# Linear-attention block on one core: the last two heads' numerators computed by tokens and carried in spare columns of the other heads

## The chip, the cores and the metric

The kernel runs on one core of a Trainium2 chip. The metric is the device time of one execution in microseconds (us). A core has five engines that run their own instruction streams: TensorE (PE) for matrix products, VectorE (DVE) and ScalarE (ACT) for elementwise work and reductions, POOL (GpSimd) for the same and for starting transfers, SP (SyncE) for starting transfers. Products land in PSUM, a memory of eight banks that VectorE and ScalarE read.

## The reference

One transformer block over S = 2048 tokens of width D = 640, with H = 32 heads of Dh = 20 and an MLP of width F = 1728:

```python
mod = (_silu(c) @ w_mod).reshape(c.shape[0], 6, 1, -1)
sa, ca, ga, sb, cb, gb = (mod[:, 0], ..., mod[:, 5])
h = _layernorm(x) * (1 + ca) + sa
# attention, on h:
pq = jnp.einsum("bhsd,hdf->bhsf", q, w_phi)             # pk from k alike
phi_q = jnp.concatenate([_softmax(pq), _softmax(-pq)], axis=-1)
kv  = jnp.einsum("bhsf,bhsd->bhfd", phi_k, v)
z   = jnp.einsum("bhsf->bhf", phi_k)
num = jnp.einsum("bhqf,bhfd->bhqd", phi_q, kv)
den = jnp.einsum("bhqf,bhf->bhq", phi_q, z)[..., None] + 1e-6
o = num / den
...
x = x + ga * (o.reshape(B, S, D) @ wo)
h = _layernorm(x) * (1 + cb) + sb
x = x + gb * (square(relu(h @ w1 + b1)) @ w2 + b2)
```

Each head has 40 features: the softmax of 20 values and that of their negatives.

## The kernel before

Tokens are worked in 16 tiles of 128 and in 8 pairs of tiles (256 tokens, `j` = 0 to 7). Large products are made from a high and a low part of each operand in three terms (high by high, high by low, low by high). All of these products, and the plain fp32 ones of `num`, are written by one helper, line 79; all subtractions that make a low part by another, line 89.

The kernel has three stretches. In the first the weights are folded and keys, values and queries are projected. There TensorE is in the order of the code and a scheduler places the other engines' work. At the end, near 255 us, kv and z of all heads are complete. The second is the attention stage, in which every engine's order is the order of the code. The third is the MLP with its `up` products and accumulators.

In the attention stage 30 heads are worked in five groups (`GR`, 0 to 4) of two halves with three heads each: 60 columns of values, and 120 of features. The last two heads are a sixth group of 40 columns of values and 80 of features. The stage does the following.

- `e_prod(t)`, `e_recip(t)` (VectorE, some on POOL) make the inverse of the denominators of tile t, and `e_scale(t)` multiplies the features by them into `ezb` (1280 columns, in one of four buffers): a pass over 1200 columns (line 905) and one over the last 80 (line 910).
- `tr_e(j, groups)` turns `ezb` by TensorE into a bank `te` (20 transposes of 120 columns, and two of 80 for the sixth group) and ScalarE copies it to `ept` (lines 927 and 929).
- `num(j)` multiplies the turned features by the masked kv (`kvd`, products of 64 columns) into three banks `numa`, `numb`, `numc`. The sixth group's kv stands three times side by side (`kv5`), so that its numerators come out in 120 rows of `numc`.
- `num_hi(j)` (ScalarE) and `num_lo(j)` (VectorE from pair 2 on, TensorE with a negative identity and ScalarE before) store `ot`, the numerators' high and low parts.
- `do_wo(j, i, h)` makes half h (384 or 256 columns) of the attention output of tile 2j + i: 16 products into `pwo`, three terms for each of five groups and one stacked product for the sixth, whose weights `WO[5]` hold high, high and low parts one under the other. ScalarE copies the result to `at` (line 986) and starts its transfer to memory.

Pair j's four `do_wo` calls alternate with the turning and the numerators of pair j + 1. VectorE does `e_scale` for tiles two or three further on. Among these stand the last four query tiles' softmax (`q_chain` with `mxq` and the subtraction at line 438 on VectorE, the exponentials `eq` at lines 441 and 442 on ScalarE), the splitting of MLP weights (`w<-rw`, `w<-rawt`, line 1018), and the first layer norm pieces of the MLP (`junk<-xm`, lines 1122 and 1127, and `xx`, line 1146). In the last pair ScalarE makes the MLP's first inputs (`xm`, `h`).

A single PSUM bank `tp` serves `numc`, then the turned MLP inputs; three banks serve `te`, `numa` and `numb`, and four the output products.

Of the kernel before, what the change touches and what calls it, by code (L numbers as in the profile page):

```python
# [15 lines left out]
P = 128  # L16
# [26 lines left out]
    *range(21),  # L43
    *range(11),
    13, 0, 2, 11, 12, 1, 3, 11, 14, 20, 15, 16, 18, 19, 17, 10, 13, 14, 0, 12,
# [7 lines left out]
def kernel(  # L53
# [347 lines left out]

    def proj(nm, t, between=None):
        p = pj(f"p{nm}{t}")
        j, i = divmod(t, 2)
        s = slice(i * P, (i + 1) * P)
        for h, (a, b) in enumerate(CUT):
            terms = []
            for d in range(NC):
                w = W[nm, d]
                terms += three(HT[j][:, d, 0, s], HT[j][:, d, 1, s], w[:, 0, a:b], w[:, 1, a:b])  # L410
            at, hook = 0, None
            if between and h == between[0]:
                at, hook = between[1:]
                mm(p[h][:, : b - a], terms[:at], last=False)
                hook()
            mm(p[h][:, : b - a], terms[at:], first=(at == 0))
        return p
# [42 lines left out]

    def do_q(t, between=None):
        q_out(t, proj("q", t, between=between))

# [25 lines left out]
    def prep_wo(g, ga_b):  # L489
        o, n = GR[g]  # L490
        t = row("s1", f"rwo{g}")
        m = P
        if g < 5:
            nc.gpsimd.memset(t, 0.0)
            for c in range(2):
                nc.sync.dma_start(t[64 * c : 64 * c + 60], wo[o + 60 * c : o + 60 * c + 60])
        else:
            m = 3 * n
            for i in range(3):
                nc.sync.dma_start(t[i * n : i * n + n], wo[o : o + n])  # L500
        w = wslot(f"wo{g}")
        WO[g] = w
        with tc.issue_after(newest(ET_.DVE)):
            nc.vector.tensor_tensor(t[:m], t[:m], ga_b[:m], op=ALU.mult)
        nc.scalar.activation(w[:m, 0], t[:m], AF.Copy)
        lo(w[:m, 1], t[:m], w[:m, 0])
        if g == 5:
            nc.gpsimd.dma_start(w[2 * n : m, 0], w[2 * n : m, 1])

# [17 lines left out]
    def wo_weights(*gs):  # L527
# [190 lines left out]
    for t in range(2, NT - 2):  # L718
# [13 lines left out]
        p = proj("v", t, (1, 0, lambda: t1(j + 1, 4)) if t == NT - 3 else None)  # L732
        if i == 0:
# [16 lines left out]
        if t < NT - POSTPONED:  # L750
            do_q(t, (1, 3, lambda: t1(j + 1, 4, more=LAST_COL.get(t))) if i else None)
# [62 lines left out]
    kv_t = flat(kvtile)  # L814
    kvd = kv_t[:120, :640].rearrange("p (g n) -> p g n", n=P)
    kv5 = kv_t[:80, 640:760]
    def make_z():
# [18 lines left out]

    q_out(q0 + 1, proj("q", q0 + 1, between=(0, 9, make_z)))

# [9 lines left out]

    def kv_out():
        for b, (g0, g1) in enumerate(((0, 4), (4, 5))):  # L850
            nc.scalar.activation(kv_t[:120, P * g0 : P * g1], kvt[b][:120, : (g1 - g0) * P], AF.Copy)
        nc.scalar.activation(
            kv5.rearrange("p (r n) -> p r n", r=3), kvt[1][:80, None, P : P + 40].to_broadcast([80, 3, 40]), AF.Copy
        )

    def kv_masks():
        k = kv_t[:120, : 5 * P].rearrange("p (g n) -> p g n", n=64)
        nc.vector.tensor_tensor(k, k, mask[:, None, :].to_broadcast([120, 10, 64]), op=ALU.mult)
        k = kv5.rearrange("p (r n) -> p r n", r=3)
        nc.vector.tensor_tensor(k, k, mask5[:, None, :].to_broadcast([80, 3, 40]), op=ALU.mult)  # L860

# [37 lines left out]

    def e_scale(t):  # L900
        if t >= NT:
            return
        dn = DN[t]
        EU[t] = EZB[t % 4]
        nc.vector.tensor_tensor(  # L905
            EU[t][:, :1200].rearrange("p (u s h d) -> p s u h d", s=2, h=3, d=DH),
            ET[t][:, :, :600].rearrange("p s (u h d) -> p s u h d", h=3, d=DH),
            dn[:, :, :30].rearrange("p s (u h) -> p s u h", h=3)[:, :, :, :, None].to_broadcast([P, 2, 10, 3, DH]), op=ALU.mult
        )
        nc.vector.tensor_tensor(  # L910
            EU[t][:, 1200:].rearrange("p (s h d) -> p s h d", s=2, d=DH),
            ET[t][:, :, 600:].rearrange("p s (h d) -> p s h d", d=DH),
            dn[:, :, 30:, None].to_broadcast([P, 2, 2, DH]), op=ALU.mult
        )

    def tr_e(j, gs):
        for g in gs:
            o, n = GR[g]
            p = bank(f"te{j}_{g}")
            t = EPT[j, g] = feat("s4", f"ept{j}_{g}")  # L920
            for i in range(2):
                for c in range(2 if g < 5 else 1):
                    a = c * 256 + i * P
                    b, m = (2 * o + 120 * c, 120) if g < 5 else (1200, 80)
                    nc.tensor.transpose(p[:m, a : a + P], EU[2 * j + i][:, b : b + m], ident)
            if g < 5:
                nc.scalar.activation(t[:120], p[:120].rearrange("p (s n) -> p s n", s=2), AF.Copy)
            else:
                nc.scalar.activation(t[:80, 0], p[:80, :256], AF.Copy)

    def num(j):
        OT[j] = ht(f"ot{j}", j)
        ps = [bank(f"numa{j}"), bank(f"numb{j}"), tp(f"numc{j}")]
        for g in range(5):
            for c in range(2):
                mm(ps[g // 2][64 * c : 64 * c + 64, (g % 2) * 256 : (g % 2) * 256 + 256],
                   [(kvd[:, g, 64 * c : 64 * c + 64], EPT[j, g][:120, c])], first=(g % 2 == 0), last=False, skip=True)
# [3 lines left out]
        OT[j, 5] = row("s3", f"ot5_{j}")[:, 80:336].bitcast(F32R)  # L941
# [14 lines left out]
    def num_lo(j):  # L956

        if j >= DIRECT:
            for b, (src, hi, low) in enumerate(num_parts(j)):
                r = GR[5][1] if b == 3 else P  # L960
                lo(low[:r], src[:r], hi[:r])
            return
        for b, (src, hi, _) in enumerate(num_parts(j)):
            r = 120 if b == 3 else P
            nc.tensor.matmul(src, neg[:r, :r], hi, start=False, stop=True, skip_group_check=True)
        for b, (src, _, low) in enumerate(num_parts(j)):
            r = GR[5][1] if b == 3 else P
            nc.scalar.activation(low[:r], src[:r], AF.Copy)

    PWO, AT = {}, {}  # L970

    def do_wo(j, i, h, a=0, b=16):
        t = 2 * j + i
# [11 lines left out]
        if b == 16:  # L985
            nc.scalar.activation(AT[t][:, cs_], PWO[t][h][:, :n], AF.Copy)
# [201 lines left out]
    for j in range(NB):  # L1188
        nxt = j + 1 < NB
        b, c = 2 * j + 5, 2 * j + 6  # L1190
        te_at = (0, 1) if 0 < j < 6 else (1, 2)
        if j == 4:
# [12 lines left out]
        load_e(b + 2)  # L1205
        def te(at):
            for i, gs in enumerate((range(3), (3, 4, 5) if te_at[0] == 0 else (5, 3, 4))):
                if nxt and te_at[i] == at:
                    tr_e(j + 1, gs)

        do_wo(j, 0, 0)
        te(0)
        if j == 5:
            exps(EQ[KEPT + 3])
            q_sums(KEPT + 3)
            e_prod(b)
        do_wo(j, 0, 1)
        if j == 7:
            t2(0, 0)
            t2(0, 1)  # L1220
        te(1)
        if j == 4:
# [12 lines left out]
        if j != 5:  # L1235
            e_recip(b)
            e_scale(b)
        do_wo(j, 1, 0)
        if j == 7:
            t2(0, 2)  # L1240
            t2(0, 3)
        te(2)
        if nxt:
            num(j + 1)
            num_hi(j + 1)
        do_wo(j, 1, 1, 0, 8)
        if j == 7:
# [6 lines left out]
        if not nxt:  # L1254
            do_wo(j, 1, 1, 8, 16)
        if nxt:
            do_wo(j, 1, 1, 8, 11)
            num_lo(j + 1)
            do_wo(j, 1, 1, 11, 16)
        if j == 5:  # L1260
# [511 lines left out]
```

## Time and profile before

| | us |
|---|---|
| median of three runs | 756.05 (755.88 to 756.07) |
| span of the profiled execution | 754.9 |
| TensorE busy | 749.6 |
| VectorE busy | 607.5 |
| ScalarE busy | 458.8 |
| POOL busy | 170.4 |
| kv and z complete (start of the attention stage) | 254 to 255 |
| first `up` product of the MLP | 386.8 |

The span runs from the first to the last instruction in the trace. The granted clock of TensorE is full throughout. In the lines of the timeline the first two numbers are start and duration in us, then engine, line and tiles; a bracket at the end is the idle time ahead and the instruction that ended it, and xN means that N such instructions are put in one row, from the first's start to the last's end.

### The profile page before, as it was taken

To read this page: it belongs to the slowest core of one execution; us is meant where nothing else is said; L and a number is where in the kernel's file an instruction comes from. 1 tells how busy PE (TensorE), PEld (TensorE's weight loads), DVE (VectorE), ACT (ScalarE), POOL (GpSimd) and SP (SyncE) were. 2 spreads that over 40 slices of the span, in tenths; PEclk is the share of its full clock that TensorE was granted. 3 is DMA by queue.
4 is the path that set the end of the run, shared out by engine and by line. 5 is a ranking of instruction groups with operands and counts; after the bars stand their busy time and mean duration, and the time that the engine had idled before them with its cause. 6 is when DMAs were issued, how large, how long until landed. Compare 5 with 4: busy or idle time off the path is not lost.

```text
span 754.9 us, 15404 instructions
## 1 busy us (share of the span) xinstructions
PE 749.6 (99%) x5888; PEld 731.9 (97%) x5888; DVE 607.5 (80%) x1123; ACT 458.8 (61%) x1060; POOL 170.4 (23%) x365
## 2 busy tenths in 40 slices
PE   9999999999999999999999999999999999999998
PEld 9999999999999998998899999999999999999997
DVE  6598987988999899999755768787777776777766
ACT  5767666677863355556677757485574756647431
POOL 3001101011200237646303030132221313213110
PEclk9999999999999999999999999999999999999999
DMA  9811431342432264664777475897677767667461
GB/s 324 336 39 80 155 96 70 106 139 103 138 105 93 71 190 142 143 153 124 173 204 218 121 216 215 278 326 204 185 213 204 205 196 212 191 181 208 132 188 36
DMA packets 58931, 126.70 MB, mean 168 GB/s; under 512 B 7452, under 2 KB 16417, under 8 KB 58857
## 3 DMA queue, kind: packets, MB, share of 16 engines
q1 hardware_dynamic: 38706, 79.41, 32.1%
q0 software_dynamic: 17568, 41.00, 22.0%
q10 hardware_dynamic: 2583, 5.30, 1.9%
q8 instruction: 46, 0.75, 0.5%
q14 instruction: 28, 0.23, 0.1%
HBM read 100.94 MB, written 29.89 MB: 173 GB/s over the span
## 4 chain that ended last, share of the span: by engine, by line
PE 86%; DVE 11%; POOL 1%; issue 1%; ACT 0%; DVEq 0%; POOLq 0%
PE up L79 24%; PE acc L79 18%; PE pk L79 9%; PE pv L79 9%; PE pq L79 8%; PE acc3x L79 5%; PE pwo L79 3%; PE kvp L455 3%; DVE dn L883 3%; DVE scr L881 2%; DVE ezb L905 2%; PE foldk L281 1%; PE ta L363 1%; DVE ot L89 1%; POOL dn L889 1%; PE foldq L281 1%
## 5 line engine op out<-in xcount | busy, mean ns | idle before, releaser
L79 PE MATMUL up<-h,w 128*128 128x256 f32 x1640 | 204.4, 276 | 0.1
L79 PEld LDWEIGHTS up<-h,w 128*128 128x128 f32 x1640 | 196.4, 188 | 0.5 <-DVE h L89 0.3
L1321 ACT ACTIVATE ft<-up,b_t 128x256 f32<-128x256 f32 x104 | 48.9, 471 | 96.0 <-PE up L79 95.6
L79 PE MATMUL acc<-w,ra 128*128 128x384 f32 x452 | 97.5, 335 | 0.0
L79 PE MATMUL pwo<-wo,ot 128*128 128x256 f32 (+3 forms) x512 | 79.9, 311 | 0.4 <-DVE ot L89 0.4
L1322 DVE TENSOR_TENSOR ft<-ft 128x256 f32<-128x256 f32 x104 | 43.8, 421 | 43.0 <-ACT ft L1321 41.4
L79 PEld LDWEIGHTS pwo<-wo,ot 128*128 128x128 f32 (+1 forms) x512 | 74.3, 188 | 3.5 <-issue 2.7
L79 PE MATMUL pq<-wq,hT 128*128 128x384 f32 (+1 forms) x480 | 75.1, 311 | 0.0
L79 PEld LDWEIGHTS acc<-w,ra 128*128 128x128 f32 x452 | 72.7, 188 | 0.9 <-DVE ra L89 0.6
L79 PE MATMUL pk<-wk,hT 128*128 128x384 f32 (+1 forms) x480 | 72.7, 308 | 0.0
L79 PE MATMUL pv<-wv,hT 128*128 128x384 f32 (+1 forms) x480 | 71.6, 306 | 0.0
L79 PEld LDWEIGHTS pq<-wq,hT 128*128 128x128 f32 x480 | 71.0, 188 | 0.6 <-issue 0.2
L79 PEld LDWEIGHTS pk<-wk,hT 128*128 128x128 f32 x480 | 70.5, 188 | 0.4 <-issue 0.2
L79 PEld LDWEIGHTS pv<-wv,hT 128*128 128x128 f32 x480 | 70.0, 188 | 0.0
L89 DVE TENSOR_TENSOR ra<-ft,ra 128x384 fp32r<-128x384 f32 (+2 forms) x86 | 36.8, 449 | 32.7 <-ACT ra L1345 19.4
L1431 POOL DMA_DIRECT2D ring_a<-td_a x34 | 18.5, 544 | 117.1 <-PE acc L79 103.7
L1345 ACT ACTIVATE ra<-ft 128x384 fp32r<-128x384 f32 x48 | 25.2, 526 | 28.5 <-DVE ft L1322 22.4
L79 PE MATMUL acc3x<-w,ra 128*128 128x256 f32 x231 | 39.5, 278 | 0.0
L79 PEld LDWEIGHTS acc3x<-w,ra 128*128 128x128 f32 x231 | 37.2, 188 | 0.0
L1336 DVE TENSOR_TENSOR ft<-ft 128x128 f32<-128x128 f32 x136 | 33.4, 286 | 1.2
L446 DVE TENSOR_REDUCE sk<-ek 128x64 f32<-128x1280 f32 x16 | 23.7, 1483 | 12.4 <-ACT ek L441 10.8
L889 POOL TENSOR_TENSOR dn<-dn,rs_q 128x32 f32<-128x32 f32 x32 | 19.9, 622 | 59.0 <-DVE dn L883 58.7
(264 smaller groups left out, 1458.2 us busy)
## 6 DMA issues: line engine op xcount, KB each, us to landing
ring_c<-td_c POOLq DMA_DIRECT2D x34, 384.0 KB, 4.1
ring_a<-td_a POOLq DMA_DIRECT2D x34, 384.0 KB, 3.5
ring_b<-td_b POOLq DMA_DIRECT2D x34, 256.0 KB, 3.5
esp<-eq SPq DMA_DIRECT2D x12, 640.0 KB, 3.2
el<-esp SPq DMA_DIRECT2D x12, 640.0 KB, 4.4
rw<-in_w SPq DMA_DIRECT2D x23, 320.0 KB, 3.5
wm<-in_w_mod SPq DMA_DIRECT2D x20, 320.0 KB, 3.7
xb<-in_x SPq DMA_DIRECT2D x8, 640.0 KB, 4.0
```

Of the source, the lines that this page charges most:

```text
L79: nc.tensor.matmul(o, a, b, start=first and i == 0, stop=last and i == len(terms) - 1, skip_group_check=skip,)
L89: (eng or nc.vector).tensor_tensor(out_lo, full, hi.bitcast(F32), op=ALU.subtract)
L281: nc.tensor.matmul(p[g // 3][:, (g % 3) * 120 : (g % 3) * 120 + n], r, bd_t[:120, g * 120 : g * 120 + n], start=True, stop=True,)
L446: nc.vector.tensor_reduce(s, heads(flat(e)), axis=AX.X, op=ALU.add)
L455: nc.tensor.matmul(kvp[g // 4][64 * c : 64 * c + 64, a : a + 2 * n].rearrange("p (s n) -> p s n", s=2), v[:, u], e[:, :, o : o + n], start ...
L883: nc.vector.tensor_reduce(dn.rearrange("p s h -> p (s h)"), heads(z), axis=AX.X, op=ALU.add)
L889: nc.gpsimd.tensor_tensor(dn[:, s], dn[:, s], rs[:, 1 - s], op=ALU.mult)
L1321: nc.scalar.activation(r, p, AF.Relu, bias=b1_t[:, f : f + 1])
L1322: nc.vector.tensor_tensor(r, r, r, op=ALU.mult)
L1336: nc.vector.tensor_tensor(t[:, o], t[:, a], t[:, b], op=op)
L1345: nc.scalar.activation(a[:, 0, :3], t[:, :3], AF.Copy)
L1431: nc.gpsimd.dma_start(RING[j, n, r], TD[n][r].bitcast(F32R))
```

## The change

The last two heads' numerators are computed with tokens as rows instead of columns. `e_scale` is split: `e_tail` writes the 80 scaled features of these heads for both tiles of a pair to a tile of its own, `ut`; `e_main` writes the other 1200 to `ezb`, now ten rows of 128 columns of which 120 are used. `tail_turn(j)` turns `ut` into the bank `tail` (the one of `numc`), and ScalarE copies it to `ept_5`. `tail_num(j)` multiplies `ept_5` (as the loaded operand) by the 40 columns of `kv5`, and ScalarE copies the 40 numerators of every token into columns 120 to 123 of the ten rows of `ezb`, four to a row. The `te` transposes take 124 columns, so the numerators are turned with the features. `kvd` gets four rows of an identity for each half, which hand them through `num` into rows 60 to 63 and 124 to 127 of each group's numerators, spare so far. The rows of `wo` for these 40 columns are loaded into the same rows of the five groups' weights. So `WO[5]`, its preparation, its slot, the sixth group's two products in `num`, its high and low parts and the 16th product of every output half are gone. The `hooks` of `do_wo` put the four steps `tail_turn`, `tail_num`, `te` of groups 0 to 2 and `te` of groups 3 and 4 between the output products: `turns` gives for each the tile of the pair, the half and the number of products ahead of it.

```diff
@@ prep_wo @@
-        m = P
-        if g < 5:
-            nc.gpsimd.memset(t, 0.0)
-            for c in range(2):
-                nc.sync.dma_start(t[64 * c : 64 * c + 60], wo[o + 60 * c : o + 60 * c + 60])
-        else:
-            m = 3 * n
-            for i in range(3):
-                nc.sync.dma_start(t[i * n : i * n + n], wo[o : o + n])
+        for c in range(2):
+            e = 600 + 4 * (2 * g + c)
+            nc.sync.dma_start(t[64 * c : 64 * c + 60], wo[o + 60 * c : o + 60 * c + 60])
+            nc.sync.dma_start(t[64 * c + 60 : 64 * c + 64], wo[e : e + 4])
...
-        13: lambda: (wo_weights(5), gb_load()),
+        13: lambda: gb_load(),
...
+    nc.gpsimd.memset(kv_t[96:, :640], 0.0)
+    nc.gpsimd.tensor_copy(
+        kv_t[96:, :640].rearrange("p (b n) -> p b n", n=64)[:, :, 60:],
+        ident[96:, None, 120:124].to_broadcast([32, 10, 4]),
+    )
...
+    def e_tail(t):
...
+        nc.vector.tensor_tensor(
+            UT[t].rearrange("p (s h d) -> p s h d", s=2, d=DH),
+            ET[t][:, :, 600:].rearrange("p s (h d) -> p s h d", d=DH),
+            DN[t][:, :, 30:, None].to_broadcast([P, 2, 2, DH]), op=ALU.mult
+        )
+    def e_main(t):
...
+        EU[t] = EZB[t % 4].rearrange("p (u n) -> p u n", n=P)
         nc.vector.tensor_tensor(
-            EU[t][:, :1200].rearrange("p (u s h d) -> p s u h d", s=2, h=3, d=DH),
+            EU[t][:, :, :120].rearrange("p u (s h d) -> p s u h d", s=2, d=DH),
...
+    def tail_turn(j):
+        p = PT[j] = tp(f"tail{j}")
+        t = EPT[j, 5] = feat("s4", f"ept{j}_5")[:80, 0]
+        for i in range(2):
+            nc.tensor.transpose(p[:80, i * P : i * P + P], UT[2 * j + i], ident)
+        nc.scalar.activation(t, p[:80, :256], AF.Copy)
+
+    def tail_num(j):
+        for i in range(2):
+            p = PT[j][:, 256 + 40 * i : 296 + 40 * i]
+            nc.tensor.matmul(p, EPT[j, 5][:, i * P : i * P + P], kv5, start=True, stop=True, skip_group_check=True)
+        for i in range(2):
+            p = PT[j][:, 256 + 40 * i : 296 + 40 * i]
+            nc.scalar.activation(EU[2 * j + i][:, :, 120:124], p.rearrange("p (u r) -> p u r", r=4), AF.Copy)
...
@@ num @@
-        for a, b in ((0, 64), (64, 120)):
-            mm(ps[2][a:b, 256:], [(kv5[:, a:b], EPT[j, 5][:80, 0])], first=False, last=False, skip=True)
@@ num_parts @@
-        return parts + [(ps[2][:120, 256:], OT[j, 5][:120], OT[j, 5][:120])]
+        return parts
@@ do_wo @@
-        terms.append((OT[j, 5][:120, s], WO[5][:120, 0, cs_]))
-        mm(PWO[t][h][:, :n], terms[a:b], first=(a == 0), last=(b == 16))
+        mm(PWO[t][h][:, :n], terms[a:b], first=(a == 0), last=(b == 15))
@@ the stage's start @@
-    e_scale(1)
+    e_tail(1)
+    kv_mask5()
+    e_main(1)
     kv_masks()
...
-    do_q(q0 + 3, (1, 8, lambda: tr_e(0, range(3))))
-    tr_e(0, (5, 3, 4))
+    do_q(q0 + 3, (1, 0, lambda: tail_turn(0)), (1, 6, lambda: tail_num(0)), (1, 12, lambda: tr_e(0, range(3))))
+    tr_e(0, (3, 4))
@@ the loop over pairs @@
-        te_at = (0, 1) if 0 < j < 6 else (1, 2)
+        turns = {1: ((0, 0, 11), (0, 0, 15), (0, 1, 4), (0, 1, 15)), 6: ((0, 1, 2), (0, 1, 8), (0, 1, 15), (1, 0, 15)),
+                 0: ((0, 1, 4), (0, 1, 10), (1, 0, 3), (1, 0, 15))}.get(j, ((0, 0, 6), (0, 0, 11), (0, 0, 15), (0, 1, 15)))
```

Three places of the resulting order bear on the prediction. The first is TensorE in pair 4, where pair 5 is turned: the end of the second tile of pair 3 (`pwo_1`), the first half of pair 4 (`pwo_0`), then `te` of pair 5. Before:

```order
L79 MATMUL pwo_1_4065<-wo_2812,ot_3_3922 128x256
L79 MATMUL pwo_0_4166<-wo_2195,ot_4084 128x384 x3
L79 MATMUL pwo_0_4166<-wo_2203,ot_4084 128x384 x3
L79 MATMUL pwo_0_4166<-wo_2405,ot_4084 128x384 x3
L79 MATMUL pwo_0_4166<-wo_2706,ot_4084 128x384 x3
L79 MATMUL pwo_0_4166<-wo_2714,ot_4084 128x384 x3
L79 MATMUL pwo_0_4166<-wo_2812,ot_4_4100 128x384
L925 MATMUL te_0_4186<-ident,ezb_3156 120x128 x2
L925 MATMUL te_0_4186<-ident,ezb_3157 120x128 x2
```

And with the change:

```order
L79 MATMUL pwo_0_4148<-wo_2196,ot_4071 128x384 x3
L79 MATMUL pwo_0_4148<-wo_2205,ot_4071 128x384 x3
L933 MATMUL tail_4157<-ident,ut_3953 80x128 x2
L79 MATMUL pwo_0_4148<-wo_2408,ot_4071 128x384 x3
L79 MATMUL pwo_0_4148<-wo_2710,ot_4071 128x384 x2
L939 MATMUL tail_4157<-kvd,ept_5_4158 128x40 x2
L79 MATMUL pwo_0_4148<-wo_2710,ot_4071 128x384
L79 MATMUL pwo_0_4148<-wo_2719,ot_4071 128x384 x3
L951 MATMUL te_0_4176<-ident,ezb_3154 124x128 x2
L951 MATMUL te_0_4176<-ident,ezb_3155 124x128 x2
```

The two products with the sixth group's weights (`ot_3`, `ot_4`) are gone, and the tail's two steps stand after six and eleven products of the half that precedes `te`.

The second place is ScalarE at the same point of the program. Before:

```order
L1018 ACTIVATE w_2_3771<-rw_2_3772 128x640
L441 ACTIVATE eq_2833<-eq_2833 128x640
L442 ACTIVATE eq_2833<-eq_2833 128x640
L986 ACTIVATE at_4168<-pwo_0_4166 128x384
L927 ACTIVATE ept_0_4187<-te_0_4186 120x512
```

With the change:

```order
L1043 ACTIVATE w_2_3760<-rw_2_3761 128x640
L442 ACTIVATE eq_2829<-eq_2829 128x640
L443 ACTIVATE eq_2829<-eq_2829 128x640
L934 ACTIVATE ept_5_4158<-tail_4157 80x256
L942 ACTIVATE ezb_3154<-tail_4157 128x10x4
L942 ACTIVATE ezb_3155<-tail_4157 128x10x4
L1011 ACTIVATE at_4150<-pwo_0_4148 128x384
L952 ACTIVATE ept_0_4177<-te_0_4176 124x512
```

The copy to `ept_5` and the two copies back to `ezb` stand behind the two exponentials of a query tile and ahead of `at`.

The third is ScalarE one pair on, where pair 6 is turned. Before:

```order
L986 ACTIVATE at_4269<-pwo_1_4268 128x256
L988 DMA a_9_213<-at_4269 128x640
L1018 ACTIVATE w_3_3952<-rawt_3953 128x640
L1127 ACTIVATE junk_4247,rn_4245<-xm_4137,smb_4244 128x640 x2
L986 ACTIVATE at_4366<-pwo_0_4364 128x384
```

With the change:

```order
L1011 ACTIVATE at_4253<-pwo_1_4252 128x256
L1013 DMA a_9_213<-at_4253 128x640
L1043 ACTIVATE w_3_3937<-rawt_3938 128x640
L1152 ACTIVATE junk_4231,rn_4229<-xm_4118,smb_4228 128x640 x2
L934 ACTIVATE ept_5_4352<-tail_4351 80x256
L942 ACTIVATE ezb_3152<-tail_4351 128x10x4
L942 ACTIVATE ezb_3153<-tail_4351 128x10x4
L1011 ACTIVATE at_4344<-pwo_0_4342 128x384
```

Here the three copies stand behind the weight's high part and the two squares of the layer norm (`junk`), again ahead of `at`.

More of the change, by code (lines that the diff above doesn't have):

```diff
@@ L43 @@
     *range(21),
-    *range(11),
+    *range(9), 10,
     13, 0, 2, 11, 12, 1, 3, 11, 14, 20, 15, 16, 18, 19, 17, 10, 13, 14, 0, 12,
@@ L400, in t1, with proj @@
             mod_sum(*more)
-    def proj(nm, t, between=None):
+    def proj(nm, t, *between):
         p = pj(f"p{nm}{t}")
@@ L410, in proj @@
                 terms += three(HT[j][:, d, 0, s], HT[j][:, d, 1, s], w[:, 0, a:b], w[:, 1, a:b])
[L411 to L416, printed above, removed]
+            done = 0
+            for k, at, hook in between:
+                if k == h:
+                    mm(p[h][:, : b - a], terms[done:at], first=(done == 0), last=False)
+                    hook()
+                    done = at
+            mm(p[h][:, : b - a], terms[done:], first=(done == 0))
         return p
@@ L459, in do_kv, with do_q @@
             )
-    def do_q(t, between=None):
-        q_out(t, proj("q", t, between=between))
+    def do_q(t, *between):
+        q_out(t, proj("q", t, *between))
     def q_out(t, p):
@@ L503, in prep_wo @@
         with tc.issue_after(newest(ET_.DVE)):
[L504 to L508, printed above, removed]
+            nc.vector.tensor_tensor(t, t, ga_b, op=ALU.mult)
+        nc.scalar.activation(w[:, 0], t, AF.Copy)
+        lo(w[:, 1], t, w[:, 0])
     ga_b = row("s4", "ga_b")
@@ L750 @@
         if t < NT - POSTPONED:
-            do_q(t, (1, 3, lambda: t1(j + 1, 4, more=LAST_COL.get(t))) if i else None)
+            do_q(t, *([(1, 3, lambda: t1(j + 1, 4, more=LAST_COL.get(t)))] if i else []))
             if norm and i:
@@ L814 @@
     kv_t = flat(kvtile)
-    kvd = kv_t[:120, :640].rearrange("p (g n) -> p g n", n=P)
-    kv5 = kv_t[:80, 640:760]
+    kvd = kv_t[:124, :640].rearrange("p (g n) -> p g n", n=P)
+    kv5 = kv_t[:80, 640:680]
+    nc.gpsimd.memset(kv_t[96:, :640], 0.0)
[3 more added lines that the diff above has]
+    )
     def make_z():
@@ L835, in make_z @@
                 nc.vector.tensor_copy(zb[:, :, 600:640], p[:, 120:200].rearrange("p (s n) -> p s n", s=2))
-    q_out(q0 + 1, proj("q", q0 + 1, between=(0, 9, make_z)))
+    q_out(q0 + 1, proj("q", q0 + 1, (0, 9, make_z)))
     kvt = [None, None]
@@ L849, in kv_out, with kv_mask5 @@
     def kv_out():
+        nc.scalar.activation(kv5, kvt[1][:80, P : P + 40], AF.Copy)
         for b, (g0, g1) in enumerate(((0, 4), (4, 5))):
             nc.scalar.activation(kv_t[:120, P * g0 : P * g1], kvt[b][:120, : (g1 - g0) * P], AF.Copy)
-        nc.scalar.activation(
-            kv5.rearrange("p (r n) -> p r n", r=3), kvt[1][:80, None, P : P + 40].to_broadcast([80, 3, 40]), AF.Copy
-        )
+    def kv_mask5():
+        nc.vector.tensor_tensor(kv5, kv5, mask5, op=ALU.mult)
     def kv_masks():
@@ L898, in e_recip @@
             nc.vector.tensor_tensor(DN[t][:, s], rs[:, 1 - s], DD[t], op=ALU.mult)
-    def e_scale(t):
+    UT = {}
+    def e_tail(t):
+        if t >= NT:
+            return
+        if t % 2 == 0:
+            u = row("s3", f"ut{t // 2}")
+            UT[t], UT[t + 1] = u[:, :80], u[:, 80:160]
+        nc.vector.tensor_tensor(
[4 more added lines that the diff above has]
+    def e_main(t):
         if t >= NT:
@@ L909, in e_scale @@
         )
[L910 to L914, printed above, removed]
+    def e_scale(t):
+        e_tail(t)
+        e_main(t)
+    PT = {}
+    def tail_turn(j):
[11 more added lines that the diff above has]
+            nc.scalar.activation(EU[2 * j + i][:, :, 120:124], p.rearrange("p (u r) -> p u r", r=4), AF.Copy)
     def tr_e(j, gs):
         for g in gs:
-            o, n = GR[g]
             p = bank(f"te{j}_{g}")
@@ L921, in tr_e @@
             for i in range(2):
-                for c in range(2 if g < 5 else 1):
+                for c in range(2):
                     a = c * 256 + i * P
[L924 to L929, printed above, removed]
+                    nc.tensor.transpose(p[:124, a : a + P], EU[2 * j + i][:, 2 * g + c, :124], ident)
+            nc.scalar.activation(t[:124], p[:124].rearrange("p (s n) -> p s n", s=2), AF.Copy)
     def num(j):
@@ L936, in num @@
                 mm(ps[g // 2][64 * c : 64 * c + 64, (g % 2) * 256 : (g % 2) * 256 + 256],
-                   [(kvd[:, g, 64 * c : 64 * c + 64], EPT[j, g][:120, c])], first=(g % 2 == 0), last=False, skip=True)
-        for a, b in ((0, 64), (64, 120)):
-            mm(ps[2][a:b, 256:], [(kv5[:, a:b], EPT[j, 5][:80, 0])], first=False, last=False, skip=True)
+                   [(kvd[:, g, 64 * c : 64 * c + 64], EPT[j, g][:124, c])], first=(g % 2 == 0), last=False, skip=True)
         NUM[j] = ps
-        OT[j, 5] = row("s3", f"ot5_{j}")[:, 80:336].bitcast(F32R)
     NUM = {}
@@ L958, in num_lo, with do_wo, wo_part @@
         if j >= DIRECT:
-            for b, (src, hi, low) in enumerate(num_parts(j)):
-                r = GR[5][1] if b == 3 else P
-                lo(low[:r], src[:r], hi[:r])
+            for src, hi, low in num_parts(j):
+                lo(low, src, hi)
             return
[L963 to L968, printed above, removed]
-    PWO, AT = {}, {}
-    def do_wo(j, i, h, a=0, b=16):
+        for src, hi, _ in num_parts(j):
+            nc.tensor.matmul(src, neg, hi, start=False, stop=True, skip_group_check=True)
+        for src, _, low in num_parts(j):
+            nc.scalar.activation(low, src, AF.Copy)
+    PWO, AT = {}, {}
+    def do_wo(j, i, h, *hooks, a=0, b=15):
+        for at, hook in hooks:
+            if at > a:
+                wo_part(j, i, h, a, at)
+            hook()
+            a = at
+        if a < b:
+            wo_part(j, i, h, a, b)
+    def wo_part(j, i, h, a, b):
         t = 2 * j + i
@@ L1190, with hooks @@
         b, c = 2 * j + 5, 2 * j + 6
-        te_at = (0, 1) if 0 < j < 6 else (1, 2)
+        turns = {1: ((0, 0, 11), (0, 0, 15), (0, 1, 4), (0, 1, 15)), 6: ((0, 1, 2), (0, 1, 8), (0, 1, 15), (1, 0, 15)),
+                 0: ((0, 1, 4), (0, 1, 10), (1, 0, 3), (1, 0, 15))}.get(j, ((0, 0, 6), (0, 0, 11), (0, 0, 15), (0, 1, 15)))
+        todo_ = (lambda: tail_turn(j + 1), lambda: tail_num(j + 1), lambda: tr_e(j + 1, range(3)), lambda: tr_e(j + 1, (3, 4)))
+        def hooks(i, h):
+            return [(at, f) for (i_, h_, at), f in zip(turns, todo_) if nxt and (i, h) == (i_, h_)]
         if j == 4:
@@ L1205 @@
         load_e(b + 2)
[L1206 to L1212, printed above, removed]
+        do_wo(j, 0, 0, *hooks(0, 0))
         if j == 5:
@@ L1216 @@
             e_prod(b)
-        do_wo(j, 0, 1)
+        do_wo(j, 0, 1, *hooks(0, 1))
         if j == 7:
@@ L1237 @@
             e_scale(b)
-        do_wo(j, 1, 0)
+        do_wo(j, 1, 0, *hooks(1, 0))
         if j == 7:
@@ L1241 @@
             t2(0, 3)
-        te(2)
         if nxt:
@@ L1245 @@
             num_hi(j + 1)
-        do_wo(j, 1, 1, 0, 8)
+        do_wo(j, 1, 1, b=8)
         if j == 7:
@@ L1254 @@
         if not nxt:
-            do_wo(j, 1, 1, 8, 16)
+            do_wo(j, 1, 1, a=8)
         if nxt:
-            do_wo(j, 1, 1, 8, 11)
+            do_wo(j, 1, 1, a=8, b=11)
             num_lo(j + 1)
-            do_wo(j, 1, 1, 11, 16)
+            do_wo(j, 1, 1, a=11)
         if j == 5:
```

8 lines of the change are left out of this document (2 added, 6 removed).

## The prediction

> **What bounds the kernel now.** I read the page's totals first, then the table of stretches over the attention stage, then the chain of waits through it, and at the places the chain names the timelines of TensorE (PE), ScalarE (ACT) and VectorE (DVE). The page:
>
> ```profile
> span 754.9 us, 15404 instructions
> PE 749.6 (99%) x5888; PEld 731.9 (97%) x5888; DVE 607.5 (80%) x1123; ACT 458.8 (61%) x1060; POOL 170.4 (23%) x365
> PE 86%; DVE 11%; POOL 1%; issue 1%; ACT 0%; DVEq 0%; POOLq 0%
> ```
>
> TensorE is busy 99% and carries 86% of the chain, so fewer products look like a shorter kernel. But 11% of the chain is VectorE's, and the stretches say where (columns: PE, PEld, DVE, ACT, POOL busy, clock, DMA share, GB/s):
>
> ```profile
> 235.00:250.00 15.00, 15.00 (x127) 14.78 (x125) 14.08 (x16) 5.42 (x15) 0.00 (x0) 1.00 0.28 93
> ...
> 277.70:332.80 55.10, 55.10 (x418) 49.44 (x417) 53.89 (x77) 28.64 (x62) 34.09 (x59) 1.00 0.54 151
> 332.80:355.00 22.20, 21.77 (x164) 19.98 (x163) 21.78 (x33) 14.39 (x31) 11.03 (x24) 1.00 0.69 156
> ...
> 390.00:410.00 20.00, 20.00 (x159) 19.57 (x158) 14.33 (x25) 15.26 (x32) 5.50 (x15) 1.00 0.84 263
> ```
>
> From 277.7 to 332.8 TensorE is busy 55.10 us of 55.10 and VectorE 53.89: the two run in step, and neither alone sets the pace. The chain of waits says which one binds:
>
> ```profile
> 331.52 1.33 DVE ot L89 x3
> ...
> 347.76 0.61 DVE ot L89
> 348.37 0.04 issue
> 348.41 2.70 PE pwo L79 x14
> 351.11 1.31 PE te L925 x12
> 352.43 1.89 PE pwo L79 x16
> 354.32 1.09 PE te L925 x10
> 355.42 2.80 PE pwo L79 x16
> ...
> 360.10 0.87 PE numc L79 x8
> ...
> 375.57 9.45 PE pwo L79 x64
> 385.04 0.49 ACT at L986
> ...
> 388.86 3.22 PE up L79 x26
> ```
>
> Up to 348.4 the end hangs on VectorE (its subtractions `ot` feed the output products `pwo`), then to 385.0 on TensorE, then on ScalarE's normalization for the MLP, whose `up` products start at 388.86. TensorE is full after that (20.00 of 20.00 from 390 to 410) so a shift at 388.86 reaches the end as it is.
>
> **The prices.** From the chain: a `pwo` product of 256 columns 1.89/16 = 0.118 us, of 384 columns 2.80/16 = 0.175, a transpose 1.31/12 = 0.109, a record of a `num` product 0.87/8 = 0.109. The groups, and two rows for fp32 products with few columns:
>
> ```profile
> L79 PE MATMUL numc<-ept,kvd 80*64 80x256 f32 x16 | 4.8, 379 | 0.0
> L79 PE MATMUL numc<-ept,kvd 80*56 80x256 f32 x16 | 4.8, 379 | 0.0
> L929 ACT ACTIVATE ept<-te 80x256 f32<-80x256 f32 x8 | 3.0, 379 | 11.0 <-PE numa L79 11.0
> ...
> 13.91 4.19 PE L281 MATMUL foldq<-bd_t,raw_q 120*128 120x120 f32 x36
> 18.03 0.85 PE L591 MATMUL mrow<-wm,cs 128*32 128x128 f32 x20
> ...
> 248.51 2.47 PE kvp L455 x43
> ```
>
> **The change part by part.** *Output products.* One of 16 goes in each half, 0.175 + 0.118 twice per pair: 0.59 us. *Numerator products of heads 30 and 31.* 16 + 16 records over 8 pairs are 4 per pair, 4 × 0.109 = 0.44 us. Their two transposes move. *Products by tokens.* Two fp32 products per pair with 128 columns loaded and 40 moved, two records each like the `num` ones. No row has this form. The low end is `kvp` (64 columns loaded, 2.47/43 = 0.057): 4 × 0.057 = 0.23. The high end is `foldq` (128 loaded, (18.03 − 13.91)/36 = 0.114): 0.46. `mrow`, with 32 loaded, takes 0.78/20 = 0.039, so the price follows the columns loaded, and `foldq` is nearest: I take 0.45. TensorE thus saves 0.59 + 0.44 − 0.45 = 0.58 us a pair, 4.6 us over eight.
>
> [...]
>
> *VectorE.* The subtraction for the 40 rows goes from pair 2 on. Its share shows in the double row:
>
> ```profile
> 332.12 0.73 DVE L89 TENSOR_TENSOR ot<-numc,ot 128x256 fp32r<-128x256 f32 x2
> 332.78 0.80 DVE L435 TENSOR_REDUCE mxq<-eq 128x32 f32<-128x640 f32 x1
> ...
> 284.27 1.49 DVE L905 TENSOR_TENSOR ezb<-el,dn 128x1200 f32<-128x1200 f32 x1
> 329.38 1.41 DVE L905 TENSOR_TENSOR ezb<-el,dn 128x1200 f32<-128x1200 f32 x1
> ```
>
> Two take 332.78 − 332.12 = 0.66, so one is 0.33. By 332.85 (331.52 + 1.33) three pairs' (2, 3, 4) are gone: 1.0 us, and that is all VectorE gives there; the mask on these heads' keys and values gets narrower and moves ahead of one scaling pass, which I cost at nothing. The scaling pass over 1200 columns now writes rows of 120 with a gap; the same form took 1.41 and 1.49 in this run, eight times from the first row to the last, so I keep its price and hold the 0.08 between them for the range.
>
> *What is free.* The sixth output weight's preparation and the five memsets go from a stretch where TensorE is full (15.00 of 15.00 between 235 and 250): nothing, in either direction. The ten 4-row loads are on SP long before use. POOL's two new instructions stand before 258.46, behind 24.8 us of idle:
>
> ```profile
> 258.46 1.42 POOL L889 TENSOR_TENSOR dn<-dn,rs_q 128x32 f32<-128x32 f32 x1 [24.80 <-DVE dn L883]
> ```
>
> If that cover were gone they would delay `dn` by well under that 1.42 each. On ScalarE a copy of 256 columns goes and two of 40 columns come per pair, each at most the 0.38 of `ept<-te 80x256` (3.0/8): they lie beside the output products behind them, and at their dearest would outlast these 0.70 us by 0.1.
>
> *The new wait.* This decides. Before the next pair's `te` transposes, TensorE must now wait for: tail transposes, ScalarE's copy `ept_5`, tail products, ScalarE's two copies back. Five to six output products stand between the steps, under 1 us. ScalarE works in program order, and at two pairs long work is queued ahead of that copy:
>
> ```profile
> 336.06 0.74 ACT L441 ACTIVATE eq<-eq 128x640 f32<-128x640 f32 x1 [1.52 <-DVE eq L438]
> ...
> 337.33 0.47 ACT L986 ACTIVATE at<-pwo 128x384 f32<-128x384 f32 x1
> ...
> 347.66 0.38 ACT L986 ACTIVATE at<-pwo 128x256 f32<-128x256 f32 x1 [0.33 <-PE pwo L79]
> ...
> 350.03 0.83 ACT L1127 ACTIVATE junk<-xm,smb 128x640 f32<-128x640 f32 x1
> 350.77 0.19 ACT L1127 ACTIVATION_READ_ACCUMULATOR junk<-xm,smb 128x1 f32 x1
> ...
> 382.25 0.38 ACT L986 ACTIVATE at<-pwo 128x256 f32<-128x256 f32 x1 [0.83 <-PE pwo L79]
> ```
>
> TensorE's own rows at these places:
>
> ```profile
> 335.60 1.48 PE L925 MATMUL te<-ident,ezb 128*120 128x128 f32 x12
> 345.52 2.46 PE L79 MATMUL pwo<-wo,ot 128*128 128x256 f32 x18
> 350.95 1.48 PE L925 MATMUL te<-ident,ezb 128*120 128x128 f32 x12
> 367.43 1.47 PE L925 MATMUL te<-ident,ezb 128*120 128x128 f32 x12
> ```
>
> *Pair 5's turn.* The exponentials wait for VectorE, so they come 1.0 earlier; the copy behind them takes the place of `at` at 337.33 − 1.0 = 336.33, ends 0.38 later and releases TensorE 0.04 later (the `issue` of 348.37): 336.75. Products 0.45, four output products 0.70: `te` at 337.90, before 335.60 (+2.3). From there to the end of `num` it was 345.52 − 335.60 = 9.92; less two transposes 0.22, two output products 0.29, four records 0.44: 8.97, so 346.87. Then 15 × 0.118 = 1.77: 348.64, and two products of 0.175: 348.99, where before the chain had 348.41 (+0.6). VectorE's saving is used up.
>
> *Pair 6's turn.* Before, `at` started 0.25 after its products' end (345.52 + 1.89 = 347.41); now at 348.89. From it to the end of the second square, 350.77 + 0.19 − 347.66 = 3.30: 352.19. Copy and hop 0.42, products 0.45, four output products 0.70: `te` at 353.76, before 350.95 (+2.8).
>
> *Pair 7's turn and the end.* Between these `te` the new transposes cancel those removed, products add 0.45, five output products (0.70) and four records (0.44) go, and normalization pieces stand ahead of the copy on ScalarE here too, with six output products between turn and products; I put 0.4 for that wait, a guess (without it the forecast is 756.9): −0.29, so +2.5 at `te` of pair 7. To `at` at 382.25 go two transposes, four output products (0.59) and four records: −1.24, leaving +1.28. The later savings lie beside ScalarE's run from 382.25 to 388.38.
>
> The profiled span is 754.9 and the median 756.05, so 1.15 lies around it: 754.9 + 1.28 + 1.15 = 757.3. With the products at 0.23, three times 0.22 less: 756.6. I forecast 757.2 (+0.15%), near the end whose price I took. I count as a change what is over 0.2%, 1.5 us, about what a measurement of this kernel can tell; so this is "the same", near its upper edge.
>
> **Rivals.** *Faster: ScalarE's queue does not hold the copies.* If exponentials and squares are ready early enough, TensorE follows VectorE: −1.0 at 348.41, then 0.22 + 0.45 − 0.175 to `te` of pair 6: −0.5; −0.69 to pair 7, −1.24 to the end: −2.4, 753.6. For it: ScalarE is busy 14.39 of 22.20 us here. Against it: 1.52 us of its idling stands exactly before the exponentials.
>
> *Faster still: TensorE alone sets the pace.* All 4.6 us come: 751.4. Against it: VectorE's 53.89 of 55.10.
>
> *Slower: VectorE does not gain its 1.0 by 332.85*, because the scaling pass into gapped rows is dearer. Eight such passes lie in the full stretch; 0.13 us more on each eats the gain, and everything behind it comes 1.0 later: 758.2. It decides from about 0.3 us, that is 0.04 a pass, half the spread between 1.41 and 1.49. For it: the first of them already cost 1.49. Against it: the same passes vary without a change of form.
>
> **How the numbers follow.** The forecast as described (756.2 to 757.56) 0.43; the slower rival, with any dearer round trip, 0.37; ScalarE not holding 0.15; all of the saving 0.05. So faster 0.20, same 0.43, slower 0.37. The range reaches from just under the first faster case to the slower rival with a little for its tail: 753.2 to 758.6, leaving out the fullest saving and some of both ends.
>
> **What would show it.** In the profile after: TensorE idle some 3 us before the tail products near 336.8 and 1 to 2 us near 352.6, released by `ept_5`; `te` of pairs 5 to 7 later by 2.3, 2.8 and 2.5; VectorE's subtractions of pair 4 ending near 331.8; `up` starting near 390.1; tail products of four records in 0.45. It is wrong if VectorE idles before 332 (the turns then bind earlier), if those waits are under 1 us, or if the subtractions of pair 4 end at 332.5 or later.

## The result, and the profile after

The changed kernel takes 760.24 us (median of 4, 760.09 to 760.65), the kernel before on the same chip 756.06 (755.88 to 756.41): a ratio of 1.0056 (95% interval 1.0042 to 1.0070). It is slower by 4.2 us. The forecast was 757.2 (753.2 to 758.6), so the time lies outside the range, on the side of the slower rival but not through it.

The page after, its span and totals, against the lines shown of before:

```profile
span 758.9 us, 15323 instructions
PE 749.2 (99%) x5854; PEld 731.0 (96%) x5854; DVE 604.2 (80%) x1115; ACT 458.7 (60%) x1065; POOL 165.4 (22%) x361
```

TensorE has 34 recorded products fewer and yet 749.2 us of work, where it had 749.6. Products that go without their time going are a sign that the remaining ones cost more. The stretches say where. The column behind POOL is the granted clock:

```profile
302.00:332.80 30.80, 30.54 (x227) 27.24 (x225) 30.29 (x44) 16.75 (x36) 17.89 (x32) 1.00 0.61 138
332.80:346.00 13.20, 10.44 (x66) 9.71 (x66) 12.75 (x17) 7.66 (x17) 2.60 (x6) 0.87 0.59 159
346.00:360.00 14.00, 12.48 (x87) 11.27 (x83) 7.83 (x13) 8.81 (x19) 7.99 (x27) 0.88 0.43 89
360.00:375.00 15.00, 14.84 (x109) 13.43 (x108) 12.24 (x17) 8.74 (x21) 5.08 (x9) 1.00 0.65 150
```

TensorE stands still for 2.76 us of the second stretch and 1.52 of the third, and in both its clock is below full, which it was nowhere in the same part of the kernel before. In slices of one microsecond:

```profile
336.00:337.00 1.00, 1.00 (x8) 1.00 (x9) 1.00 (x2) 0.30 (x2) 0.00 (x0) 1.00 1.03 346
337.00:338.00 1.00, 1.00 (x9) 0.97 (x8) 0.93 (x6) 0.70 (x2) 0.78 (x3) 0.81 1.05 335
338.00:339.00 1.00, 1.00 (x7) 1.00 (x6) 1.00 (x1) 0.80 (x2) 0.92 (x2) 0.50 0.11 26
...
340.00:341.00 1.00, 1.00 (x6) 1.00 (x6) 1.00 (x2) 0.00 (x0) 0.00 (x0) 0.50 0.00 0
341.00:342.00 1.00, 1.00 (x11) 1.00 (x10) 1.00 (x1) 0.03 (x1) 0.00 (x0) 0.98 0.00 0
...
354.00:355.00 1.00, 1.00 (x7) 0.96 (x7) 0.36 (x1) 0.52 (x3) 0.94 (x1) 0.85 0.46 165
355.00:356.00 1.00, 1.00 (x7) 1.00 (x6) 0.00 (x0) 0.74 (x2) 0.80 (x5) 0.50 0.03 8
```

The clock falls to exactly half, and not in the wait but after it. Finer slices put the two half-clock stretches at 337.63 to 341.04 and 354.69 to 358.10: 3.41 us each at a clock of 0.50, which cost 1.7 us of full-speed work apiece. TensorE's own timeline at the three turns (brackets: idle time ahead and what ended it):

```profile
331.97 1.12 PE L79 MATMUL pwo<-wo,ot 128*128 128x384 f32 x5
335.85 0.64 PE L939 MATMUL tail<-kvd,ept 80*128 80x40 f32 x4 [2.76 <-ACT ept L934]
336.32 0.94 PE L79 MATMUL pwo<-wo,ot 128*128 128x384 f32 x4
337.10 2.25 PE L951 MATMUL te<-ident,ezb 128*124 128x128 f32 x12
339.00 2.93 PE L79 MATMUL pwo<-wo,ot 128*128 128x256 f32 x15
...
347.66 3.02 PE L79 MATMUL pwo<-wo,ot 128*128 128x256 f32 x21
...
353.30 0.64 PE L939 MATMUL tail<-kvd,ept 80*128 80x40 f32 x4 [1.52 <-ACT ept L934]
...
354.56 2.63 PE L951 MATMUL te<-ident,ezb 128*124 128x128 f32 x12
...
371.04 0.64 PE L939 MATMUL tail<-kvd,ept 80*128 80x40 f32 x4 [0.16 <-ACT ept L934]
...
372.42 1.47 PE L951 MATMUL te<-ident,ezb 128*124 128x128 f32 x12
```

The twelve `te` records take 2.25 and 2.63 us behind the two long waits and 1.47 behind the short one, as before the change. The 15 output products of 256 columns behind the first take 2.93, where 16 took 2.08 at this place before:

```profile
336.83 2.08 PE L79 MATMUL pwo<-wo,ot 128*128 128x256 f32 x16
```

The end of the stage, from the chain of waits:

```profile
385.92 0.40 ACT at L1011
...
392.43 3.67 PE up L79 x30
```

The chain's `up` products start 3.57 us later than the 388.86 of before. The profiled execution is the slowest of the four; its span is 4.0 longer, and the remaining 0.4 us lie behind `up`, in the MLP. There this chain holds one late transfer (`ring_b`, 6.94 us, where the median is 3.6):

```profile
507.95 6.94 DMA ring_b<-td_b
```

That it makes the 0.4 us is not shown: TensorE stands still for only 0.13 us there (busy 7.87 of the 8.00 us from 508 to 516), and from the chain's `up` to the end the profiles of all ten kernels here take between 365.8 and 366.5 us, so 0.4 is within the spread of that stretch.

### The profile page after: what moved, and what is told of

It is laid out like the page before. It is cut to its first block, busy times and chain, and to the rows that moved or that the text cites. A ratio compares the mean times of both kernels' runs of the same rounds, so it can differ in the third digit from the quotient of the medians.

```text
span 758.9 us, 15323 instructions
## 1 busy us (share of the span) xinstructions
PE 749.2 (99%) x5854; PEld 731.0 (96%) x5854; DVE 604.2 (80%) x1115; ACT 458.7 (60%) x1065; POOL 165.4 (22%) x361
## 4 chain that ended last, share of the span: by engine, by line
PE 84%; DVE 10%; ACT 2%; POOL 2%; issue 1%; DMA 1%; ACTq 0%; POOLq 0%
PE up L79 23%; PE acc L79 17%; PE pk L79 9%; PE pv L79 9%; PE pq L79 8%; PE acc3x L79 5%; PE pwo L79 3%; PE kvp L456 3%; DVE dn L881 2%; DVE scr L879 2%; DVE ezb L917 2%; PE te L951 1%; PE foldk L281 1%; DMA ring_b<-td_b 1%; PE ta L363 1%
## 5 line engine op out<-in xcount | busy, mean ns | idle before, releaser
L79 PE MATMUL pwo<-wo,ot 128*128 128x384 f32 (+1 forms) x480 | 79.9, 318 | 0.3 <-DVE ot L89 0.3
L79 PEld LDWEIGHTS pwo<-wo,ot 128*128 128x128 f32 x480 | 70.9, 193 | 3.5 <-issue 2.7
L340 POOL TENSOR_SCALAR sma<-sma 128x2 f32<-128x2 f32 x6 | 1.7, 284 | 137.3 <-ACT xb L339 137.3
```

The costliest lines, as they stand in the source:

```text
L79: nc.tensor.matmul(o, a, b, start=first and i == 0, stop=last and i == len(terms) - 1, skip_group_check=skip,)
```

## The experiments

The theory: each of the two long waits costs its length, and because TensorE stood still in it, a stretch of 3.41 us at half clock follows (a window, in the expectations), 1.7 us more. The rival: the half clock comes from something else at these places. The DMA engines are full there (share 1.03 to 1.11 from 332 to 338), so transfers were the first suspect. In the kernel before, the same ten microseconds from 332 to 342 have a DMA share of 0.85, above the changed kernel's 0.65, at full clock. The "before" of each ratio is the kernel before, run beside it.

**The waits filled.** Ahead of the tail products, output products whose results go to unused columns:

```diff
+    def keep(j):
+        n = {5: 23, 6: 12}.get(j + 1, 0)
+        if n:
+            mm(PWO[2 * j][1][:, 256:512], [(OT[j][:, 0, 0, :P], WO[0][:, 0, :256])] * n, skip=True)
...
-        todo_ = (lambda: tail_turn(j + 1), lambda: tail_num(j + 1), lambda: tr_e(j + 1, range(3)), lambda: tr_e(j + 1, (3, 4)))
+        todo_ = (lambda: tail_turn(j + 1), lambda: (keep(j), tail_num(j + 1)), lambda: tr_e(j + 1, range(3)), lambda: tr_e(j + 1, (3, 4)))
```

> The changed kernel with the two long waits filled: 23 output products of 256 columns (2.7 us) into unused columns of a bank ahead of pair 5's tail products, 12 (1.4 us) ahead of pair 6's. The waits stay, TensorE is busy in them; the results of the added products are not used. Theory (TensorE falls to half clock for one window of 3.4 us because it stood still, 1.7 us lost each time): no half clock, 756.8 us (756.4 to 757.2). Rival (the half clock comes from something else at that place, such as the transfers that fill the DMA engines there, or the loss is the waits alone): the half clock stays, 760.2 us (759.9 to 760.6).

Measured: 757.19 us (10 runs), ratio 1.0015 (1.0005 to 1.0024). Its stretch of ten microseconds round pair 5's turn (columns as above):

```profile
332.00:342.00 10.00, 9.90 (x80) 9.62 (x79) 9.83 (x13) 5.49 (x12) 2.40 (x5) 1.00 0.65 146
```

TensorE's timeline of that turn, with the 23 added products in the first row:

```profile
332.47 3.72 PE L79 MATMUL pwo<-wo,ot 128*128 128x384 f32 x28
336.29 0.64 PE L944 MATMUL tail<-kvd,ept 80*128 80x40 f32 x4
...
337.54 1.47 PE L956 MATMUL te<-ident,ezb 128*124 128x128 f32 x12
```

The tail products start no earlier than in the changed kernel (336.29; 335.85 there), so the time of the wait is not won back, but the clock is full, `te` takes 1.47, and 3.05 us of the median are gone with more work done (3.4, if each kernel is set against the kernel before that ran beside it). The DMA share of the stretch, 0.65, is what it is in the changed kernel, whose clock over the same stretch is 0.83:

```profile
332.00:342.00 10.00, 7.24 (x45) 6.89 (x44) 9.83 (x12) 4.71 (x11) 2.11 (x4) 0.83 0.65 148
```

So at these places it is TensorE's standing still, not the transfers, that brings the half clock.

**The exponentials moved.** Only the order on ScalarE at pair 5's turn:

```diff
         do_wo(j, 0, 0, *hooks(0, 0))
+        if j == 4:
+            exps(EQ[KEPT + 2])
...
             q_chain(KEPT + SPREAD[j], False)
-            if j > 1:
-                exps(EQ[KEPT + SPREAD[j]])
```

> The changed kernel with one move: the two exponentials of the query tile of pair 4 stand behind the tail's copies on ScalarE, not ahead. Theory: pair 5's wait of 2.76 us and its half clock go; VectorE's order then sets the pace at about 346.0 (4.5 us of work regained, of it 3.6 by then), pair 6's wait stays at 1.3 to 1.5 us: 755.8 us if its half clock stays too, 754.1 if that wait is just short enough. Rival (half clock from another cause than the wait): 757.5 us.

Measured: 754.66 us (753.30 to 755.56, 10 runs), ratio 0.9975 (0.9966 to 0.9984). The one move takes away more than the change had cost, and the time lies between the two that were expected, 755.8 and 754.1. The mean clock is 0.999 or 1.000 in all ten executions, and pair 6's wait for `ept_5` is gone too, which I had not expected: TensorE now arrives early and waits for VectorE instead, 1.09 us, and ScalarE is through with the two squares in the meantime.

```profile
346.23 0.97 PE L79 MATMUL pwo<-wo,ot 128*128 128x384 f32 x4 [1.09 <-DVE ot L89]
...
348.43 0.64 PE L939 MATMUL tail<-kvd,ept 80*128 80x40 f32 x4
```

**Both moved.** The squares go behind pair 6's copies as well:

```diff
+        if j == 5:
+            next(ln0)
+            next(ln0)
+            next(ln0)
...
-        if j == 4:
-            next(ln0)
-            next(ln0)
-            next(ln0)
```

> As the run before, and the two squares of the layer norm (with the small copies behind them) also stand behind pair 6's tail copies on ScalarE. Theory: both long waits and both half-clock windows go, the `te` of pair 6 starts near 348.8 instead of 354.6: 752.8 us (752.0 to 754.0), faster than before the change. Rival (half clock from the transfers at that place): still two windows at half clock, 756.2 us.

Measured: 753.77 us (753.62 to 754.89, 6 runs), ratio 0.9967 (0.9955 to 0.9980): 2.6 us under the kernel before, and 6.5 under the changed kernel's median. From it TensorE's waits at the last two turns:

```profile
346.46 0.96 PE L79 MATMUL pwo<-wo,ot 128*128 128x384 f32 x4 [1.17 <-DVE ot L89]
...
349.65 1.47 PE L951 MATMUL te<-ident,ezb 128*124 128x128 f32 x12
...
364.47 0.64 PE L939 MATMUL tail<-kvd,ept 80*128 80x40 f32 x4 [0.16 <-ACT ept L934]
```

I had expected 752.8 and `te` of pair 6 at 348.8. It starts at 349.65: VectorE's subtractions let the products behind them start at 346.46, not 346.0, and the rest is the row of steps behind them. Since the second move adds little to the first (the intervals overlap), 0.9 us between the medians is not shown.

**The squares alone.** The other half of the pair: the squares move as above, the exponentials stay where the change has them.

> The changed kernel with only the two squares (and the small copies behind them) moved behind pair 6's tail copies on ScalarE; the exponentials stay ahead of pair 5's. Theory (each long wait costs its length and a window at half clock of 1.7 us): pair 5's 2.76 us and its window stay, pair 6's 1.5 and its window go: 757.0 us (756.6 to 757.5). Rival (the second half-clock window was no matter of its wait): 758.7 us.

Measured: 757.07 us (756.57 to 757.73, 10 runs), ratio 1.0007 (0.9998 to 1.0016), where 757.0 was expected. Pair 5's wait of 2.70 us stays and with it one half-clock stretch (mean clock 0.997 or 0.998 in all ten executions, 0.995 in the changed kernel's four); pair 6's is gone with its half clock:

```profile
335.69 0.64 PE L939 MATMUL tail<-kvd,ept 80*128 80x40 f32 x4 [2.70 <-ACT ept L934]
...
336.93 2.62 PE L951 MATMUL te<-ident,ezb 128*124 128x128 f32 x12
...
351.58 0.54 PE L939 MATMUL tail<-kvd,ept 80*128 80x40 f32 x4
...
352.73 1.47 PE L951 MATMUL te<-ident,ezb 128*124 128x128 f32 x12
```

**A wait put into the kernel before.**

```diff
-        do_wo(j, 0, 0)
+        if j == 4:
+            do_wo(j, 0, 0, 0, 11)
+            nc.tensor.transpose(PWO[8][1 - 0][:, 384:512], EQ[KEPT + 2][:, 1, :P], ident)
+            do_wo(j, 0, 0, 11, 16)
+        else:
+            do_wo(j, 0, 0)
```

> The kernel before, with one wait put in: in pair 4, behind 11 products of its first half, TensorE turns 128 columns of the query tile whose exponentials are still to come into unused columns of a bank (not used afterwards), so it stands still some 2.7 us there. Theory: the wait is followed by a window at half clock; 2.3 of the 2.8 us of wait and transpose come through, and 1.7 for the clock: 760.1 us (759.5 to 760.6). Rival (a wait costs only its length): 758.4 us (757.9 to 758.8).

Measured: 759.65 us (758.20 to 760.34, 5 runs), ratio 1.0036 (1.0023 to 1.0050). Both predictions were right, each in some executions: 758.20 and 758.60 with a mean clock of 0.999, and 759.65, 759.91 and 760.34 with 0.997 or 0.998. The profiled one is of the first kind; that a stretch at half clock is what the three others have is read from their mean clock alone. The profiled one stands still 2.62 us and goes on at full clock:

```profile
337.45 0.33 PE L1213 MATMUL pwo<-ident,eq 128*128 128x128 f32 x1 [2.62 <-DVE scr L881]
337.53 1.12 PE L79 MATMUL pwo<-wo,ot 128*128 128x384 f32 x5
338.49 1.48 PE L925 MATMUL te<-ident,ezb 128*120 128x128 f32 x12
```

Here the releaser named, VectorE, is the one that came last by the profile; the transpose also waits for ScalarE's exponentials, which end at the same 337.39 us.

**The same wait, filled.** 21 products ahead of that transpose:

```diff
             do_wo(j, 0, 0, 0, 11)
+            mm(PWO[8][1][:, 256:512], [(OT[4][:, 0, 0, :P], WO[0][:, 0, :256])] * 21, skip=True)
```

> The kernel before with the wait of the fourth run, and 21 output products of 256 columns (2.5 us, results not used) ahead of it, so that TensorE works where it stood. Theory: only the length of the wait is left: 2.0 to 2.4 us over the kernel before on the same chip, in every execution, and no execution with a lowered mean clock, where the unfilled wait gave both. Rival (the spread of that run had another cause): times as spread as there, up to 4 us over.

Measured: 758.73 us (758.05 to 759.38, 6 runs), ratio 1.0030 (1.0019 to 1.0041), 2.35 over the kernel before beside it, all with a clock of 0.999 or 1.000. What is left is the length of the wait; the upper group of the run above, with its lower mean clock, is gone. The transpose starts when it did in the run above, and here the releaser named is the exponential:

```profile
337.47 0.33 PE L1214 MATMUL pwo<-ident,eq 128*128 128x128 f32 x1 [0.23 <-ACT eq L442]
```

**The moves without the change.** The same two moves in the kernel before:

```diff
         do_wo(j, 0, 0)
         te(0)
+        if j == 4:
+            exps(EQ[KEPT + 2])
+        if j == 5:
+            next(ln0)
+            next(ln0)
+            next(ln0)
...
-            if j > 1:
-                exps(EQ[KEPT + SPREAD[j]])
...
-        if j == 4:
-            next(ln0)
-            next(ln0)
-            next(ln0)
```

> The kernel before, with the same two moves on ScalarE (exponentials of pair 4 and squares behind the copies `ept` of groups 0 to 2). Theory: in the kernel before TensorE doesn't wait for what stands behind them, so nothing changes: within 0.4 us of the kernel before on the same chip. Rival (the moves by themselves are what made the third run fast): 2.5 us faster than before.

Measured: 756.40 us against 756.38, ratio 0.9998 (0.9989 to 1.0007). The moves are worth nothing without the new wait.

**The last wait.** The first four `xx` pieces behind pair 7's copies, on top of both moves:

```diff
+            next(ln0)
...
-        if j == 5:
-            next(ln0)
```

> The changed kernel with the moves of the third run, and the first four normalization pieces (`xx`) moved behind pair 7's tail copies as well. Theory: the last wait, 0.16 us, goes too, nothing else changes: 753.6 us (753.2 to 754.0), 0.3% under the kernel before. Rival: the pieces are needed earlier by VectorE's turning of the MLP inputs, and the time goes up to 754.5 us.

Measured: 754.53 us (753.60 to 754.85, 6 runs), ratio 0.9971 (0.9959 to 0.9982). No gain over both moves. The rival's 754.5 was met, but not for the reason I gave: the pieces now delay ScalarE's `ept` copies, and `numb` waits for them.

```profile
372.29 1.08 PE L79 MATMUL numb<-ept,kvd 124*64 124x256 f32 x8 [0.73 <-ACT ept L952]
```

## Why the prediction was wrong

*The step that failed* is "The new wait", in both its turns. It found the waits: forecast were some 3 us near 336.8 and 1 to 2 near 352.6, released by `ept_5`; the trace has 2.76 at 335.85 and 1.52 at 353.30. But each wait was charged with its length alone, and what followed with full-clock durations. "From there to the end of `num` it was 9.92", less 0.95, gave 8.97; the trace has 347.66 − 337.10 = 10.56, 1.6 more. From `te` of pair 6 to that of pair 7 it gave 16.48 − 0.29 = 16.19; the trace has 372.42 − 354.56 = 17.86, 1.7 more. The kernel before could show neither: its clock is 1.00 throughout that stage, where the longest wait is 0.43. Of the forecast's signs of being wrong, waits under 1 us and subtractions of pair 4 that end at 332.5 or later did not come, and none of its signs was for this step.

*The tail's price* was right: from the first tail product to the next output product are 336.32 − 335.85 = 0.47, forecast 0.45 from `foldq`. The forecast has no term for the wider transposes, 124 loaded columns for 120, and at full clock none is seen: the chain after has twelve `te` records of pair 7 in 1.31 us, as before.

*VectorE's gain* was put too low, 1.0 us at pair 4; the subtractions there end at 330.96, not 332.85, which is 1.9. The three subtractions give 1.0 of it, as forecast, and 0.45 is there when the first of the eight scaling passes starts (283.82 for 284.27). Most of the rest is in the scaling: 0.24 for `ut` and 1.37 for the rest at 284, where it was 1.49 and 0.21. From its start to the next instruction the scaling of a tile takes 1.62 us before and 1.54 after at the first four passes, and 1.54 or 1.55 both before and after at the last four. The slower rival, that the gapped rows cost more, is thereby wrong. From the chain before:

```profile
284.27 1.49 DVE ezb L905
285.76 0.21 DVE ezb L910
```

And from the chain after:

```profile
283.82 0.24 DVE ut L906
284.06 1.37 DVE ezb L917
...
329.43 1.53 DVE ot L89 x3
330.96 0.72 DVE mxq L436
```

Hence `te` of pair 5 came 1.5 us late, not 2.3; behind the half clock those of pairs 6 and 7 came 3.6 and 5.0 late, not 2.8 and 2.5. *The third wait*, the guess of 0.4, was 0.16.

Together, at the chain's `up`: 390.1 as forecast, about 0.9 less for VectorE, 0.2 less for the third wait, 3.4 more for two half-clock stretches: 392.4, and the trace has 392.43. In the median the same sum gives 759.6, against 760.24 measured; the 0.6 us left are not explained. In the profile 0.4 of them lie behind `up`, where the kernels' profiles spread by 0.7.

*The faster rival* was right in its mechanism. With ScalarE's queue out of the way TensorE follows VectorE, for 753.8, where 753.6 had been worked out. That the two are so near is in part luck: the products behind VectorE's subtractions start 1.95 us earlier than before (346.46 for 348.41), where the rival counted 1.0, and the chain's `up` is 2.99 earlier, where it counted 2.4. Of the 4.6 us of TensorE's work that the forecast counted as saved, 2.6 arrive in that version. At 346.46 TensorE waits 1.17 us for VectorE; where the whole of the rest goes was not traced.

The forecast had no term for the granted clock. In the trace the two half-clock stretches are 3.41 us long and start 17.06 us apart (five times 3.41), and the one after the kernel's last product starts at 757.46, which is 123 lengths of 3.413 us after the first. (The kernel before has one there too, from 754.44 to its end; up to there its clock is full.) Ahead of the second stretch, a wait of 1.52 us was enough.

## What to carry to other kernels

When a change makes TensorE wait where it had not waited, count the wait, and as a second term the half-clock stretch that may follow: 1.7 us here for waits of 1.5 and 2.8 us. Before accepting a round trip through ScalarE, read what stands ahead of its copies in program order; moving two exponentials behind them was worth 5.6 us of median in this kernel (5.9 against the kernel before beside each). Where the order cannot be moved, filling the wait with products that nobody reads gave back about 3 us.

## What the runs showed of the hardware

Both long waits were followed by half clock in all four executions of the changed kernel, by its mean clock of 0.995, and pair 5's in all ten of the run with the squares moved, by 0.997 or 0.998; the wait of 2.62 us put into the kernel before was so in three of five, by the same two figures. So the length of a wait alone does not decide. In the changed kernel the three starts of half clock lie a whole number of steps of 3.413 us apart. How such steps cut the wait may be what differs between these five; with one trace of them this is not shown. Counted in such steps from each trace's half-clock edges, these steps were followed by half clock: one with 1.64 us of standing still (the changed kernel, 334.21 to 337.63), one with 1.52 (351.28 to 354.69), and one with 2.03 in the run with the squares moved (333.66 to 337.07). These were not: 1.12 (the changed kernel, 330.79 to 334.21), and about 1.7 in the wait put into the kernel before, whose 2.62 us are cut into about 0.9 and 1.7 by steps counted back from where its half clock starts behind the last product, 755.60. By this count the sum of standing still in a step does not decide either, since 1.52 was followed by half clock and 1.7 was not; what does is not shown. The steps that were followed by it also hold the tail's products of 40 columns, 0.64 us as recorded; no run tested whether these matter.
